# Attention denominators by accumulating DMAs, a ring of three operand tiles and more of the last inverse transform on TensorE, on one Trainium2 core

## The chip, the core and the metric

The kernel runs on one core of one Trainium2 chip. The profile shows five engines that work at the same time and wait for each other by semaphores: TensorE (PE, matrix products; the profile shows its weight loads as PEld), VectorE (DVE), ScalarE (ACT), GpSimd (POOL) and SyncE (SP). In the kernel before, PE, DVE, ACT and POOL are busy for 378.5, 360.7, 274.6 and 16.8 us of a span of 398.5 us. The page counts the transfers against 16 DMA engines. In this kernel SP issues almost all DMAs (228 of the 235 in the trace of before), one after the other, and an issue that waits for a semaphore holds up those behind it.

The metric is the device time of one execution in microseconds (us), lower is better. Each run here is four executions of a kernel, unless said otherwise, beside executions of the kernel before on the same chip. A ratio is the mean time of one kernel's fast runs over the mean of the fast runs of the kernel before in the same rounds, so it is not quite the ratio of the medians that are quoted. An execution is in the state "slow" when it took more than 1.5% longer than the fastest of the same kernel; ratios leave those out.

## The reference, cut to what matters

```python
# q, k, v: (4 batches, 8 heads, 768, 64); 16 centroids per head; x: (4, 768, 512)
mask   = argmax(q_n @ c_n.T)[:, None] == argmax(k_n @ c_n.T)[None, :]   # same cluster
scores = where(mask, (q @ k.T) / 8, -1e9)
p      = exp(scores - max)
attn   = p / (p.sum(-1) + 1e-9)               # <- the denominators of this study
x      = concat_heads(attn @ v)               # (4, 768, 512)
x1, x2, x3 = split(x @ w_proj, 3)
y      = x1 * irfft(rfft(x2) * rfft(filter)) * x3    # along the 768 rows
out    = y @ w_out
```

## The kernel before: the parts that matter

The kernel is not written in the order in which it runs. It describes operations (engine, estimated cost, due time, what it reads and writes), and a planner in Python orders them on every engine before anything is built. Constants of that planner (`T0`, `margin`, `b0` and others) therefore decide the order. The work is 16 pairs of heads (two heads share the 128 partitions). For each pair PE computes scores in six key tiles, ACT takes the exponential, PE multiplies with the values, and DVE adds the six exponential tiles up, so that only a sum over the 128 partitions is left for the denominators. PE does that sum by a matmul with ones:

```python
def acc(e, t=t):                                   # DVE, 1.75 us, five per pair
    T.nc.vector.tensor_tensor(T.acc[:], P_(t[0]), P_(t[1]) if len(t) == 2 else T.acc[:], op=Alu.add)
...
def den(e):                                        # PE: sum over partitions, line 691
    for hp in range(2):
        for ch in range(2):
            z = 2 * hp + ch
            T.nc.tensor.matmul(ap(h)[32 * z:32 * z + 32, :384], T.ones32,
                               T.acc[:, hp, ts(ch, 384)], start=True, stop=True)
...                                                # ACT copies to T.den, then SP, in order:
T.nc.sync.dma_start(T.dd[os], T.den[0:128:32])     # to HBM
T.nc.sync.dma_start(T.dn, T.dd[os].rearrange(...)) # back, spread over 128 partitions
T.nc.vector.reciprocal(T.dn, T.dn)                 # DVE
T.nc.sync.dma_start(T.dr[os].rearrange(...), T.dn) # to HBM
T.nc.sync.dma_start(T.rb[...], T.dr[os][hp:hp + 1].to_broadcast([64, S]))  # twice
```

`rb` then scales the value product into `xT`, the operand of the projection. The cluster mask gets into the scores as 16 extra rows of the score operands. The operand is called `aug`; its mask rows come from `ohT` (the one-hot cluster numbers, transposed) by eight small DMAs for each group of two pairs, also on SP.

```python
def masks(n, prs, due):
    ...
    op(("SP", .6), lambda e, ...: dma(e)(
        T.augs[aset][pr][hp][j][64 - 64 * hp:80 - 64 * hp], T.ohT[r0:r0 + 16]), due + .3 * hp,
        r=[("ohT", pr), ("zero", aset, pr, j)], w=[("augm", aset, pr, hp, j)], byts=25e3)
```

After the last pair follows a tail of about 50 us: the gating of the last batch, with inverse transforms (`I`) on PE whose even and odd parts DVE combines, and the output.

The softmax here doesn't subtract the row's maximum and nothing guards it: scores larger than these inputs give would overflow.

## Time and profile before

| | before |
|---|---|
| time, median of 3 (range) | 400.61 us (399.87 to 401.47) |
| profiled span | 398.5 us |
| PE busy, idle | 378.5 us, 20.0 us |
| DVE, ACT, POOL busy | 360.7, 274.6, 16.8 us |

PE is busy for 95% of the span and the chain of waits puts 89% of the span on PE. The next view cuts the span at the ends of the first, the sixth and the sixteenth pair's value products: head, pairs 2 to 6, pairs 7 to 16, tail. After each window comes its length, the busy time of each engine with its number of instructions, the granted clock, and the DMA engines' share.

```profile
0.00:44.90 44.90, 35.71 (x266) 18.88 (x268) 39.10 (x72) 33.79 (x67) 16.79 (x55) 1.00 0.93 175
44.90:133.60 88.70, 88.19 (x730) 44.87 (x727) 78.21 (x87) 72.02 (x133) 0.00 (x0) 1.00 0.48 111
133.60:348.80 215.20, 215.20 (x2033) 117.34 (x2037) 205.55 (x262) 154.41 (x292) 0.00 (x0) 1.00 0.28 75
348.80:398.50 49.70, 39.43 (x429) 23.85 (x427) 37.88 (x67) 14.36 (x27) 0.00 (x0) 0.94 0.16 65
```

From 133.6 to 348.8 us PE has no idle time that the profile shows (215.20 of 215.20), while DVE is busy for 95.5% of it. The groups of instructions give the ones-matmul (line 691; count, busy us, mean ns), and the waits of PE (total us, times, longest):

```profile
L691 PE MATMUL bank<-acc,ones 128*32 128x384 f32 x128 | 13.6, 498 | 0.0
```

```profile
PE bank L549 <- DMA qkraw<-in_q_dram: 5.1, 1, 5.1
PE bank L68 <- DVE y L860: 3.5, 2, 3.3
...
PE bank L68 <- DMA aug<-ohT: 0.4, 1, 0.4
```

Apart from a first load and one wait in the tail (for `y`, 3.3 us), PE waits for nothing over 1 us.

### The profile page before, as it was taken

What the parts mean: (1) busy time and instruction counts of PE and PEld (TensorE: products, weight loads), DVE (VectorE), ACT (ScalarE), POOL (GpSimd) and SP (SyncE); (2) the same over time, 40 slices, a digit from 0 to 9 for tenths busy, and PEclk for the clock granted to TensorE, in tenths of its full rate; (3) what the DMA queues carried; (4) which work ended last, traced back from release to release, by engine and by line L of the source; (5) the groups of instructions that cost most, each with busy time, mean ns of one, the idle gap of its engine ahead of it and who ended that gap; (6) DMA issues with size and microseconds to landing.
All of it is one profiled execution on the core that took longest, in us unless ns stands there. A gap on an engine that the chain in (4) does not pass through costs nothing.

```text
span 398.5 us, 8781 instructions
## 1 busy us (share of the span) xinstructions
PE 378.5 (95%) x3447; PEld 204.9 (51%) x3447; DVE 360.7 (91%) x485; ACT 274.6 (69%) x518; POOL 16.8 (4%) x55
## 2 busy tenths in 40 slices
PE   3988999999999999999999999999999999999963
PEld 3543555554445555665455555665455465555731
DVE  8889896996899999999799999999889999989981
ACT  5897889798865886768764886778865667532412
POOL 8700000000000000000000000000000000000000
PEclk9999999999999999999999999999999999999988
DMA  9939959154512415134712414111512010100304
GB/s 177 227 62 226 199 118 234 41 130 116 138 42 61 120 26 114 33 86 141 225 42 58 123 26 103 44 56 52 189 43 60 2 42 3 43 2 7 153 2 159
DMA packets 67233, 37.09 MB, mean 93 GB/s; under 512 B 56700, under 2 KB 62328, under 8 KB 67192
## 3 DMA queue, kind: packets, MB, share of 16 engines
q1 hardware_dynamic: 62856, 33.62, 33.5%
q0 software_dynamic: 1056, 2.10, 2.9%
q10 hardware_dynamic: 3280, 0.82, 1.2%
q8 instruction: 27, 0.44, 0.5%
q14 instruction: 14, 0.11, 0.1%
HBM read 30.66 MB, written 6.48 MB: 93 GB/s over the span
## 4 chain that ended last, share of the span: by engine, by line
PE 89%; ACT 4%; DMA 2%; DVE 2%; issue 1%; ACTq 0%; SPq 0%
PE bank L68 34%; PE pair L668 31%; PE bank L770 5%; PE bank L539 4%; PE bank L691 3%; PE bank L66 3%; PE bank L567 3%; ACT p L657 2%; PE bank L434 2%; DMA qkraw<-in_k_dram 1%; PE bank L580 1%; PE bank L549 1%; DMA aug<-ohT 1%; ACT p L654 1%; PE bank L460 1%
## 5 line engine op out<-in xcount | busy, mean ns | idle before, releaser
L668 PE MATMUL pair<-p,vraw 128*64 128x385 f32 x768 | 141.8, 490 | 1.0 <-ACT qkT L244 1.0
L657 ACT ACTIVATE p<-bank 128x512 f32<-128x512 f32 x192 | 113.3, 608 | 30.2 <-PE bank L68 26.7
L678 DVE TENSOR_TENSOR acc<-p,acc 128x1536 f32<-128x1536 f32 x64 | 112.2, 1754 | 6.6 <-ACT p L657 4.5
L668 PEld LDWEIGHTS pair<-p,vraw 128*64 128x64 f32 x768 | 52.2, 136 | 48.4 <-issue 40.9
L68 PE MATMUL bank<-aug,aug 128*64 128x256 bf16 (+3 forms) x654 | 69.9, 326 | 0.5 <-DMA aug<-ohT 0.4
L654 ACT ACTIVATE p<-bank 128x512 f32<-128x512 f32 x96 | 58.2, 606 | 3.0 <-PE bank L68 2.9
L68 PEld LDWEIGHTS <-aug 128*64 128x64 bf16 (+1 forms) x654 | 36.0, 110 | 31.5 <-issue 16.1
L68 PE MATMUL bank<-xT,wpj 128*64 128x384 bf16 x480 | 48.0, 326 | 0.0
L68 PEld LDWEIGHTS <-wpj 128*64 128x64 bf16 x480 | 26.9, 109 | 20.8 <-issue 11.5
L244 ACT COPY qkT<-bank 128x384 f32<-128x384 f32 x55 | 25.1, 485 | 16.1 <-PE bank L539 6.2
L678 DVE TENSOR_TENSOR acc<-p,p 128x1536 f32<-128x1536 f32 x16 | 28.0, 1750 | 4.4 <-ACT p L657 4.4
L244 ACT CAST aug<-qkT 64x768 bf16<-64x768 f32 x36 | 30.0, 833 | 2.5 <-DVE qkT L246 1.7
L68 PEld LDWEIGHTS <-y 128*64 128x64 bf16 x416 | 21.0, 112 | 15.6 <-issue 4.7
L794 DVE TENSOR_TENSOR tm<-bank,hm 128x512 f32<-128x512 f32 x44 | 27.9, 681 | 0.0
L68 PE MATMUL bank<-wout,y 128*64 128x512 bf16 x160 | 21.2, 405 | 3.5 <-DVE y L860 3.5
L770 PE MATMUL bank<-wpj,xT 128*64 128x512 bf16 x192 | 22.8, 379 | 0.0
L244 ACT COPY ob<-bank 128x512 f32<-128x512 f32 x18 | 10.3, 586 | 16.3 <-PE bank L68 15.4
L683 ACT COPY osb<-pair 128x770 f32<-128x770 f32 x16 | 12.8, 802 | 12.0 <-PE pair L668 11.7
L539 PE MATMUL bank<-ident,qkraw 128*128 128x128 f32 x144 | 20.0, 280 | 0.0
L539 PEld LDWEIGHTS bank<-ident,qkraw 128*128 128x128 f32 x144 | 15.5, 140 | 8.5 <-issue 4.1
L783 DVE TENSOR_TENSOR uv<-tm,bank 128x512 bf16<-128x512 f32 x24 | 15.3, 682 | 4.0 <-PE bank L770 2.1
L770 PEld LDWEIGHTS <-xT 128*64 128x64 bf16 x192 | 10.7, 110 | 10.8 <-issue 3.1
(146 smaller groups left out, 429.2 us busy)
## 6 DMA issues: line engine op xcount, KB each, us to landing
vraw<-in_v_dram SPq DMA_DIRECT2D x16, 384.0 KB
qkraw<-in_q_dram SPq DMA_DIRECT2D x30, 192.0 KB
qkraw<-in_k_dram SPq DMA_DIRECT2D x30, 192.0 KB
rb<-dr SPq DMA_DIRECT2D x30, 192.0 KB
out_dram<-ob SPq DMA_DIRECT2D x11, 512.0 KB
y<-in_moe_filter_fft_dram SPq DMA_DIRECT2D x4, 384.0 KB
wpj<-in_moe_w_proj_dram POOLq DMA_DIRECT2D x1, 1536.0 KB, 12.3
aug<-ohT SPq DMA_DIRECT2D x60, 24.0 KB
```

The costliest lines, as they stand in the source:

```text
L66: return T.nc.tensor.matmul(out, lhsT, rhs, start=start, stop=stop)
L68: T.nc.tensor.matmul(out[64 * i:64 * i + 64], lhsT[:, 64 * i:64 * i + 64], rhs, start=start, stop=stop)
L244: T.nc.scalar.copy(out, in_)
L539: T.nc.tensor.transpose(bank(h.ids[i // 3])[:, ts(i % 3, 128)], raw(s, i), T.ident)
L654: T.nc.scalar.activation(o, ap(h).rearrange("p (a b) -> p a b", a=2), Act.Exp, scale=0.125)
L657: T.nc.scalar.activation(flat(s)[:, lo:lo + 512], ap(h), Act.Exp, scale=0.125)
L668: T.nc.tensor.matmul(o[64 * hp:64 * hp + 64, ch, :385], T.vraw[vs][:, hp, sk * D:(sk + 1) * D], T.p[slots[sk]][:, hp, 384 * ch:384 * ch + ...
L678: T.nc.vector.tensor_tensor(T.acc[:], P_(t[0]), P_(t[1]) if len(t) == 2 else T.acc[:], op=Alu.add)
L683: op(("ACT", .83), lambda e: T.nc.scalar.copy(T.osb[os], two(ob)[:, :, :385]), te, r=[ob], w=[("osb", os)], free=[ob])
L770: T.nc.tensor.matmul(ap(h)[64 * i:64 * i + 64], T.xT[xs][:, kt, c:c + 64], T.wpj[:, kt, DM:2 * DM], start=kt == 0, stop=kt == ND - 1)
L783: op(("DVE", .68), lambda e, m=m, e_=e_, o_=o_, h=h: T.nc.vector.tensor_tensor(T.uv2[:, e_, m], T.tm[m % 2][:, 0], ap(h), op=o_), due + 1, ...
L794: op(("DVE", .68), lambda e, i=i, cs=cs, r=r, h=h: T.nc.vector.tensor_tensor(T.tm[r][:, cs], ap(h), hmrow(i, (0, 2, 2, 3)[2 * r + cs]), op ...
```

## The change

Its intent is to take work from the bound engine. Of the 16 ones-matmul passes 14 go: three accumulating DMAs fold the partitions from 128 to 16 (64, 32 and 16 rows are added onto the lower ones), the rest goes through HBM, and a small DVE reduction adds the 16 rows. There are two `acc`, so that the next pair's sums needn't wait, and three output copies `osb`. To make room in SBUF (the on-chip memory; the kernel's tiles there have up to 128 partitions) the score operands become a ring of three for pairs, in place of two sets of two. The planner also chains the scores, so that they stay in their own order. The weights are loaded in four quarters. In the tail PE forms the sums and differences of the inverse transform itself (doubled matmuls, with a negated table), and POOL may take some sums from DVE. The planner's constants were set anew, so that the order of PE's work differs throughout. The core of the diff:

```diff
-    T0 = 9.454
-    TAU1 = 3.31
-    TAU2 = 3.644
+    T0 = 12.158
+    TAU1 = 3.211
+    TAU2 = 3.472
+    def ring(n, pr):
+        return (2 * n + pr) % 3
 ...  (further constants: bonus, margin, shape, b0, w0, w1, LEAD, BUSY)
-        op(("PE", .68), den, te + 0.5, r=["acc", "ones"], w=[h], alloc=h, kind="den")
+        late = n == NG - 1                 # the last two pairs keep the ones-matmul
+        if late:
+            ...
+                flat_ = lambda: T.acc[os][:].rearrange("p a b -> p (a b)")
+                rows = 64
+                while rows >= ROWS:        # ROWS = 16
+                    op(("POOL", .8), lambda e, rows=rows: T.nc.gpsimd.dma_start(
+                        flat_()[:rows], flat_()[rows:2 * rows], accum_op=Alu.add), te, ...)
+                    rows //= 2
+                op(("SP", .6), lambda e: T.nc.sync.dma_start(T.dd[os], flat_()[:ROWS]), ...)
+                op(("SP", .6), lambda e: T.nc.sync.dma_start(T.dp, T.dd[os].rearrange("r (p b) -> p r b", b=12)), ...)
+                def gather(e):
+                    T.nc.vector.tensor_reduce(T.dn, T.dp[:].rearrange("p r b -> p b r"), axis=AX, op=Alu.add)
+                    T.nc.vector.tensor_scalar(T.dn, T.dn, EPS * S, None, op0=Alu.add)
 ...
-    T.augs = [[[[tl([128, S], BF16, ...) for j in range(2)] for hp in range(2)] for pr in range(2)] for i in range(2)]
+    T.augs = [[[tl([128, S], BF16, ...) for j in range(2)] for hp in range(2)] for i in range(3)]
 ...  (weights: one DMA of w_proj becomes four; tail: below)
+                if last:
+                    for cs in range(2):
+                        for g in range(2):
+                            for e_ in range(2):
+                                for n in range(2):
+                                    columns(bk(hh, cs)[...], T.y[:, 2 if n else e_, cs, ts(dt, 128)],
+                                            T.neg[:, cs, n] if e_ and g else T.inv[:, e_, cs, n], e_ + n == 0, e_ + n == 2)
+                    return
```

## The prediction

> **What bounds it now.** TensorE. The page gives PE 378.5 us busy of 398.5 (95%), DVE 360.7, ACT 274.6. By windows of 25 us, PE is 25.00 of 25 in every window from 100 to 350 us, at full clock; DVE is at 24.4 to 24.9 in the windows that hold gating work (125-175, 225-275, 300-350). The chain of waits gives PE 89% of the span. PE idles about 10 us before 100 us (loads, first masks) and about 10 us after 375 us (3.3 us waiting for DVE's y2 at 381.8-385, then copies and output DMA after the last matmul).
>
> **Removed.** The ones-matmul over partitions (L691 in the groups): 13.6 us busy in 16 passes. In the timeline a pass keeps the next matmul away for 0.78 us, and the matmuls before it run out 0.10 us later than usual[...]: 0.88 us. Fourteen of sixteen go: 12.3 us of PE. ACT loses about 14 copies of 0.49 us. In the tail DVE loses eight sums of 0.55 us and hands four of 0.68 us to POOL: 7 us.
>
> **Added.** Per pair: three accumulating DMAs (64, 32, 16 rows), two DMAs through HBM, a short DVE reduction and addition (estimate 0.45 us from the 0.55 us reduction of 384 and 0.15 us small operations; 6 us in all). In the tail the inverse sums double: four more groups of 16 matmuls, 0.65 us each, 2.6 us of PE. Costed by the built order with the trace's durations, PE work falls about 10.5 us in all, DVE about 6; DVE work up to the last attention pair is unchanged.
>
> **The DMA chain.** [...] From wout's 5.7 us to landing (512 KB) and small writes of about 2.4 us here, I estimate 25-30 us from last sum to operand. The order allows for it: between the last value product of a batch and the first projection it now holds 34-42 us of PE work, against 19-24 before. So I expect PE rarely to wait for it. The second acc keeps the sums from waiting.
>
> **On the critical path.** Nearly all 12.3 us lie where PE is saturated, but:
> - After the sixth pair the order holds about 214 us of PE and 214 us of DVE work (before: 216 and 200). DVE becomes a co-limit; I allow 2-4 us of new PE idling.
> - Tail: DVE falls by 7 us, PE work after the last value product rises from 37 to 40 us, so the tail turns PE-bound and keeps its length (±2).
> - The ring of three and weights by quarters make room and smooth loads; worth 0-2 us before 100 us (the 3.7 us mask DMA on the chain at 87 us may go).
>
> **Prediction.** 400.6 - 12.3 + 2.6 - 2 (tail wait) - 1 (head) + 3 (DVE bubbles) = 391 us; I put 390.5, range 383 to 398. Faster by over 2%: 0.62; within 2%: 0.33; slower: 0.05.
>
> **What would show it.** L691 left with two passes; PE busy near 368-370; last value product at 335-340 us (348.8 now); no large PE wait on rb or xT; DVE over 93% busy; the wait on y2 before the last projection under 2 us.
>
> **What would make it wrong.** Accumulating DMAs that take 10 us each, so that DVE waits for a free acc or PE for xT; loads stuck in SP's in-order queue behind the denominators' DMAs, or POOL's queue stuck on the filter wait (22 us now) before the first pair's accumulation[...]; more DVE bubbles than 4 us.

The sum comes to 390.9 us. The prediction took that the three accumulations run one after the other, on which its estimate of 25-30 us also rests; no trace of the kernel before shows it. In the trace of the change they do: POOL waits 116.3 us in all, 25 times, for an earlier accumulation (`acc<-acc`). POOL's sums: in the change the four took 1.27 us each.

## More of the kernel before

The page of the profile gives, in this order: busy time of each engine; the busy share in 40 slices of the span, in tenths, for PE and for the clock that PE was granted; what the software queue of DMAs carried; and the chain of work that ended last, by engine.

```profile
PE 378.5 (95%) x3447; PEld 204.9 (51%) x3447; DVE 360.7 (91%) x485; ACT 274.6 (69%) x518; POOL 16.8 (4%) x55
PE   3988999999999999999999999999999999999963
PEclk9999999999999999999999999999999999999988
...
q0 software_dynamic: 1056, 2.10, 2.9%
...
PE 89%; ACT 4%; DMA 2%; DVE 2%; issue 1%; ACTq 0%; SPq 0%
```

## The result and the profile after

| | before | after |
|---|---|---|
| time, median of 4 (range) | 401.04 us (399.87 to 401.88) | 417.27 us (416.34 to 418.74) |
| ratio, 95% interval | | 1.041 (1.0366 to 1.0454) |
| profiled span | 398.5 us | 414.9 us |
| PE busy, idle | 378.5, 20.0 us | 379.4, 35.5 us |
| DVE, ACT, POOL busy | 360.7, 274.6, 16.8 us | 358.5, 277.0, 55.0 us |

The result is correct and 4.1% slower. The same lines of the page, the same stages (ends of the first, sixth and sixteenth pair), the group of the ones-matmul and PE's waits for the kernel after:

```profile
PE 379.4 (91%) x3357; PEld 214.4 (52%) x3357; DVE 358.5 (86%) x491; ACT 277.0 (67%) x515; POOL 55.0 (13%) x102
PE   3878969997997999998999899999998999989994
PEclk9998998999999899999999999999999999989998
...
q0 software_dynamic: 3344, 11.73, 19.3%
...
PE 48%; DVE 22%; DMA 9%; ACT 7%; issue 7%; SPq 5%; ACTq 0%; DVEq 0%
```

```profile
0.00:45.50 45.50, 34.22 (x238) 18.36 (x240) 38.01 (x73) 31.04 (x60) 16.15 (x55) 0.96 0.92 178
45.50:140.10 94.60, 84.20 (x633) 44.07 (x631) 75.34 (x81) 71.57 (x130) 13.30 (x17) 0.96 0.73 138
140.10:365.00 224.90, 218.73 (x1985) 125.08 (x1983) 208.98 (x280) 159.23 (x296) 20.53 (x26) 1.00 0.56 109
365.00:414.90 49.90, 42.21 (x511) 26.88 (x507) 36.19 (x59) 15.15 (x29) 5.02 (x4) 0.93 0.19 73
```

```profile
L711 PE MATMUL bank<-acc,ones 128*32 128x384 f32 x16 | 1.7, 498 | 1.1 <-DVE acc L696 1.1
```

```profile
PE bank L72 <- DMA aug<-ohT: 7.5, 6, 2.9
PE bank L560 <- DMA qkraw<-in_q_dram: 5.9, 2, 5.5
PE bank L70 <- DMA aug<-ohT: 3.7, 2, 2.3
```

The ones-matmul did shrink from 128 records to 16, that is from 16 passes to 2. Yet PE is as busy as before, and idle for 15.5 us more. The chain of waits no longer runs on PE alone: DVE has 22%, DMA 9%, SP's queue 5%. (DVE's share is no sign of the loss: in `e5b_noaccum` below, the same order without the loss, it is 20%, with DMA at 2%.) The largest new wait of PE is for the masks, `aug<-ohT`: 7.5 + 3.7 us where there were 0.4. Against the kernel before, the time is lost from the second to the sixth pair (94.6 us against 88.7) and from the seventh to the sixteenth (224.9 against 215.2). The software queue carried 11.73 MB in place of 2.10.

The timeline of the second longest of these waits (start, duration, engine, line, operation; in brackets the idle time before it and what ended it; lines between are left out):

```profile
129.70 0.77 POOL L731 DMA_DIRECT2D acc<-acc  x1 [6.76 <-DMA acc<-acc]
130.17 4.71 SPq L456 DMA_DIRECT2D aug<-ohT  x6
...
134.64 0.76 POOL L731 DMA_DIRECT2D acc<-acc  x1 [4.17 <-DMA aug<-ohT]
134.83 0.10 PEld L70 LDWEIGHTS <-aug 80*128 80x128 bf16 x1 [2.55 <-DMA aug<-ohT]
134.87 0.38 PE L70 MATMUL bank<-aug,aug 80*128 80x512 bf16 x1 [2.34 <-DMA aug<-ohT]
```

An accumulating DMA starts at 129.70 us. The mask DMAs are issued from 130.17 us on, and PE's first score of that pair comes only at 134.87 us, after 2.34 us of idling that a mask DMA ended. The clock records of the trace grant PE half its rate (0.5) from 135.1 us for 3.413 us. Ahead of this window stood 2.34 us of wait, and 2.94 us ahead of another such window at 63.4 us; in the 3.413 us before these two windows PE was busy for 1.07 and 1.18 us. In the traces of before and after the changes of the granted clock are whole multiples of 3.413 us apart. I counted, over the 19 traces and from 26 us on, the windows of this grid at full rate by how long PE was busy in them: of 43 under 1.38 us all were followed by half rate, of 27 from 1.38 to 2.0 us 12, of 75 from 2.0 to 2.72 us 4, of 1905 above none (in before and after alone: 5 of 5, 2 of 2, 0 of 7, 0 of 201). So these two waits can each have cost up to 1.7 us more (an estimate: half of 3.413 us); of the eight waits for masks in this trace, these two were followed by such a window.

How tight is the order? From the built order of PE and mean durations from the trace I worked out how much PE work stands between the transposes that make `ohT` and the first score that needs the masks made of it, for the seven groups of two pairs:

```
us of PE work    g1    g2    g3    g4    g5    g6    g7
before         21.8   6.2  12.6   8.2  13.6   8.1  12.5
after          12.2   4.9   6.0   4.9   5.7   5.7   8.5
```

Into that time must fit a copy of `ohT` (0.99 us on ACT), up to eight mask issues (0.59 us each) and the landing of the last one. Four issues with the copy and a landing of 1.9 us (the median without accumulations, below) are 5.3 us by this estimate: in five of its seven groups the order after has next to no reserve, so that a landing of 3 us, or an issue that is held, shows as idle PE.

### The profile page after: what moved, and what is told of

Same layout as the page of the kernel before. It is cut to its first block, busy times and chain, and to the rows that moved or that the text cites. A ratio compares the mean times of both kernels' runs of the same rounds, so it can differ in the third digit from the quotient of the medians.

```text
span 414.9 us, 8661 instructions
## 1 busy us (share of the span) xinstructions
PE 379.4 (91%) x3357; PEld 214.4 (52%) x3357; DVE 358.5 (86%) x491; ACT 277.0 (67%) x515; POOL 55.0 (13%) x102
## 3 DMA queue, kind: packets, MB, share of 16 engines
q1 hardware_dynamic: 90060, 36.20, 38.1%
q0 software_dynamic: 3344, 11.73, 19.3%
## 4 chain that ended last, share of the span: by engine, by line
PE 48%; DVE 22%; DMA 9%; ACT 7%; issue 7%; SPq 5%; ACTq 0%; DVEq 0%
PE bank L72 17%; PE pair L682 15%; DVE acc L696 8%; DMA aug<-ohT 5%; PE bank L809 4%; SPq L456 4%; PE bank L70 3%; PE bank L550 3%; DVE tm L833 2%; ACT p L671 2%; PE bank L579 2%; DMA qkraw<-in_q_dram 2%; DVE xT L777 1%; ACT aug L255 1%; DMA rb<-dr 1%
## 5 line engine op out<-in xcount | busy, mean ns | idle before, releaser
L682 PE MATMUL pair<-p,vraw 128*64 128x385 f32 x768 | 147.5, 500 | 1.6 <-DVE inv L257 1.1
L696 DVE TENSOR_TENSOR acc<-p,acc 128x1536 f32<-128x1536 f32 x64 | 111.7, 1745 | 5.4 <-ACT p L671 2.8
L682 PEld LDWEIGHTS pair<-p,vraw 128*64 128x64 f32 x768 | 56.0, 139 | 51.5 <-issue 44.5
L72 PE MATMUL bank<-aug,aug 80*64 80x512 bf16 (+3 forms) x602 | 72.1, 330 | 9.2 <-DMA aug<-ohT 7.5
L731 POOL DMA_DIRECT2D acc<-acc x42 | 33.6, 800 | 274.3 <-DVE acc L696 144.8
L72 PEld LDWEIGHTS <-aug 80*64 80x64 bf16 (+1 forms) x602 | 37.0, 110 | 39.4 <-issue 25.0
L72 PEld LDWEIGHTS <-wpj 128*64 128x64 bf16 x480 | 28.7, 109 | 17.8 <-issue 8.9
L72 PEld LDWEIGHTS <-y 128*64 128x64 bf16 x472 | 23.0, 110 | 12.8 <-issue 4.5
L70 PE MATMUL bank<-aug,aug 80*128 80x512 bf16 (+3 forms) x83 | 19.3, 322 | 6.4 <-DMA aug<-ohT 3.7
L257 DVE COPY qkT<-bank 128x384 f32<-128x384 f32 x18 | 9.5, 553 | 12.7 <-PE bank L550 12.7
L777 DVE SCALAR_TENSOR_TENSOR xT<-osb,rb 128x768 bf16<-128x768 f32 x15 | 15.2, 1014 | 5.7 <-DMA rb<-dr 5.6
```

The source lines that it names most:

```text
L70: return T.nc.tensor.matmul(out, lhsT, rhs, start=start, stop=stop)
L72: T.nc.tensor.matmul(out[64 * i:64 * i + 64], lhsT[:, 64 * i:64 * i + 64], rhs, start=start, stop=stop)
L682: T.nc.tensor.matmul(o[64 * hp:64 * hp + 64, ch, :385], T.vraw[vs][:, hp, sk * D:(sk + 1) * D], T.p[slots[sk]][:, hp, 384 * ch:384 * ch + ...
L696: T.nc.vector.tensor_tensor(T.acc[os], P_(t[0]), P_(t[1]) if len(t) == 2 else T.acc[os], op=Alu.add)
L731: op(("POOL", .8), lambda e, rows=rows: T.nc.gpsimd.dma_start(flat_()[:rows], flat_()[rows:2 * rows], accum_op=Alu.add), te, r=[], w=[("ac ...
L777: op(("DVE", .6 if last else 1.05), lambda e, a_=a_: T.nc.vector.scalar_tensor_tensor(xv()[:, a_], osv()[:, a_], eps(), ap(rk[a_.start])[: ...
```

## The experiments

Three theories to start with:
- A, order: the new planner constants put the masks too late, whatever the DMAs do.
- Q, queue: SP is held by the waits of the denominators' chain, and the masks stand behind them.
- C, contention: the accumulating DMAs load the DMA engines, and the masks land later.

"Same order" below means that the order of PE, DVE and ACT was checked to be that of the parent kernel, so that nothing else moved. Several kernels give a wrong result.

### 1. Orders planned anew (five kernels, none settled it)

`e1_margin` sets one constant of the planner back (`margin` from 0.005 to 0.43), `e4_masks_earlier` plans the clusters 8 us earlier (`b0 = end - 31.5`), and `e2_den_on_pe` brings the ones-matmul back for all pairs:

```diff
-        late = n == NG - 1
+        late = True
```

> Edit: the changed kernel with the scheduler's margin for TensorE back at 0.43 us (it is 0.005 in the change). In the built order the PE work between the transposes of a head group's one-hot rows (ohT) and the first score of that group grows from 4.9-12 us (mostly under 6) to 8-24 us. Theory A (the new order leaves no slack between ohT, eight serial mask DMAs and the scores that need them[...]): PE idle falls from 35 us towards 20 us, the half-rate windows inside the span go, time 388 to 398 us. Theory B (mask DMAs are held in SP's in-order queue by the denominators' DMAs that wait for their chain) and theory C (traffic of the accumulating DMAs slows the masks and loads): the chain and traffic stay, so time stays at 410 us or more.

> Edit: the changed kernel with all denominators summed by matmuls with ones, as before the change (no accumulating DMAs, no dp, no gather); ring, score chain, quarters, tail and constants as in the change. PE work rises by 12 us. The scheduler, given this, leaves 6 to 15 us of PE work between ohT and the first score. A, B and C all expect it to be faster than the changed kernel in spite of the added PE work: 398 to 406 us, PE wait on mask DMAs under 5 us in all. If it stays at 412 us or more, the loss lies in the ring, the score chain, the quarters or the constants, not in the denominators' DMAs.

> Edit: the changed kernel with one constant moved: routing similarities are due 8 us earlier (end - 31.5 for end - 23.515). The built order then holds 6.6 to 16 us of PE work between ohT and the first score (4.9 to 12 in the change). Theory A: time 395 to 407 us and mask waits under 8 us. Theories B and C: within 1% of the changed kernel, 413 to 420 us.

Measured, all correct: 420.25 us (ratio 1.0533), 421.94 us (1.0545) and 427.54 us (1.0664). None came out as theory A expected. e4 missed every range; e1's time lies in the range named for the other two theories (410 us or more); e2 took the branch "412 us or more", which by its own words lays the loss on the ring, the score chain, the quarters or the constants. I don't read it so: e5b below keeps all of these in the unchanged order and takes 397.92 us. In e1 and e4 PE's waits for masks did fall, to 0.2 and 1.6 us, and both kernels were slower than the change: theory A lost its support as the whole cause. Other waits appeared in their place, for exponentials above all (6.1 us in e1, 6.3 in e4 on line 72). In e2 PE waited 7.6 us once for a table of the gating and 8.9 us for `y`, and the tail took 61.3 us instead of 49.9. What follows is a lesson of method: each of these edits made the planner reorder everything, and the new order brought losses of its own that are as large as the effect in question.

Two later kernels say the same. `e9_old_consts` is the change with all planner constants of before; `e8_den_pe_old_consts` is that with the ones-matmul back as well, so that of the change only the ring of three, the three copies, the weights by quarters and the tail stay.

> The change without its DMA denominators: ring of three operand tiles, three output copies, weights by quarters and the new tail stay, the denominators of every pair are summed on PE as before, the planner's constants are those of before. Correct result. If ring, quarters and copies cost nothing and gain nothing, this is as the tail alone: 395-399 us, L691 again in 16 passes, ohT to first score with 9 to 14 us of PE work between, mask waits under 2 us. If the ring of three itself makes the mask waits (a tile is free later), 402-410 us with aug<-ohT among PE's waits above 5 us.

> The whole change with the planner's constants of before; correct result; PE order differs: PE work between the transposes of ohT and the first score that needs it is 28, 47, 37, 5.5, 5.1, 5.5, 5.1 us for the seven head groups (after: 12.2, 4.9, 6.0, 4.9, 5.7, 5.7, 8.5). Theory (contention and queue act only where an order is tight): no PE wait on masks over 0.5 us in groups 1 to 3, waits of 1 to 3 us in some of groups 4 to 7, time 403-415 us. Rival (the new constants are what is wrong, not the DMAs): no waits on masks over 1 us at all, time 388-398 us.

Measured, both correct: e8 418.91 us (1.0469), e9 436.69 us (1.0904). In e8 there is no accumulating DMA and PE doesn't wait for masks, but 8.3 us once for a table on DVE and 5.7 us in the tail for `y`. In e9 PE waited 4.8 us for masks and more for exponentials (7.0 us in one group alone), so neither theory's number came. e8's time is outside both of its ranges too. From here on I only changed kernels without letting the order move.

### 2. Queue and contention, in the unchanged order after (four cells)

`e3_no_chain_waits`: the chain's DMAs on SP copy constant data, so that SP waits for nothing in the chain; the accumulating DMAs stay.

```diff
-  T.nc.sync.dma_start(T.dd[os], flat_()[:ROWS])
+  T.nc.sync.dma_start(T.dd[os], T.wpj[:ROWS, :2]...)       # likewise dp, dr, rb
```

`e5b_noaccum`: the 42 accumulating DMAs are left out, the chain's waits stay (and a constant added to the sums becomes 1.0). `e5_no_waits_no_accum`: both edits.

```diff
-  op(("POOL", .8), lambda e, rows=rows: T.nc.gpsimd.dma_start(..., accum_op=Alu.add), te, ...)
+  op(("POOL", .8), lambda e: None, te, ...)
```

> Edit: the changed kernel, same order of instructions on every engine, but the four kinds of denominator DMA on SP copy constant data (weights, q) in the same shapes, so that SP never waits for the accumulation, the gather or each other; wrong result on purpose. Theory B: masks and loads get out earlier, PE wait on masks falls to under 5 us, time 395 to 406 us. Theory A: the masks wait mostly for ohT itself and for their own eight serial issues, so time falls by less than a third of the loss, 409 to 416 us. Theory C: traffic stays, 412 to 418 us.

> Edit: the previous run without waits (e3), and the 42 accumulating DMAs left out as well; same order of instructions on every engine; wrong result on purpose. Theory C (traffic of the accumulating DMAs slows masks, loads and weight of everything else): a further gain of 4 us or more over e3 (409.95), to 397-405 us. Theory B (only the waits on SP's queue count): same as e3 within 1%, 406 to 412 us.

> Fourth cell of the two by two (SP's chain waits with/without, accumulating DMAs with/without), same order on every engine as after, wrong result on purpose: the 42 accumulating DMAs are left out, SP keeps its waits for the chain dd, dp, dn, dr, rb. Contention theory (the accumulating traffic lengthens the mask DMAs' landings): median landing of aug<-ohT falls from 3.0 us to about 2 us, and the time falls by about as much as between the two kernels without chain waits (12.6 us), to 403-406 us. Queue theory (SP is held behind the chain whatever the traffic): mask landings fall but PE still waits for masks 5 us or more in all, time 408-412 us. If the queue is held mainly because the accumulations make the chain slow, the two overlap: time 397-402 us, mask waits under 2 us.

| ratio to before (95% interval) | accumulating DMAs | none |
|---|---|---|
| SP waits for the chain | 1.041 (1.0366 to 1.0454), the change | 0.9946 (0.9917 to 0.9974), e5b |
| SP doesn't wait | 1.0216 (1.0166 to 1.0265), e3 | 0.9915 (0.9888 to 0.9943), e5 |

The medians are 417.27 and 397.92 us in the first row, 408.69 (three fast runs; the fourth, 416.64, was slow) and 397.37 us in the second. The trace gives the landing of the mask DMAs, from issue, as minimum, median and maximum of those it could match (44 of 60 in each). In the order after, e3, e5b, e5:

```profile
DMA to landing us min/median/max: 1.8/3.0/8.4
```

```profile
DMA to landing us min/median/max: 1.8/3.1/7.4
```

```profile
DMA to landing us min/median/max: 1.8/1.9/3.6
```

```profile
DMA to landing us min/median/max: 1.8/1.9/3.6
```

And the queue's own waits, first of the kernel after, then of e5b (SP's queue, what it waited for, total us, times, longest):

```profile
SPq L745 <- DVE dn L744: 57.4, 12, 9.8
SPq L737 <- DMA dd<-acc: 30.0, 12, 3.8
```

```profile
SPq L744 <- DVE dn L743: 64.7, 12, 10.9
SPq L736 <- DMA dd<-acc: 23.6, 12, 3.3
```

What follows:
- The accumulating DMAs are what makes the change slow in this order: without them it takes 4.5% less time (ratio 1.041 to 0.9946), whether or not SP waits it ends below the kernel before, and the view of PE's waits shows none for masks (it leaves out gaps under 0.15 us). e5b has PE idle for 21.4 us, where the change has 35.5. By stages, with the order unchanged, 12.9 of the 18.7 us lie in pairs 2 to 6 and 5.1 in pairs 7 to 16 (e5b in the view that was used above):

```profile
46.50:128.20 81.70, 79.78 (x633) 42.84 (x631) 72.41 (x78) 70.33 (x130) 0.00 (x0) 1.00 0.53 115
128.20:348.00 219.80, 217.84 (x1987) 122.44 (x1983) 211.01 (x284) 158.63 (x297) 0.00 (x0) 1.00 0.36 84
```

- They act as contention: the mask landing is 1.9 us without them and 3.0 or 3.1 us with them, and that doesn't depend on SP's waits. The loads of `vraw` and `q` land later too (medians 4.4 and 3.7 us in e5b, 5.3 and 4.4 in the change). The page of the change counts the software queue, which carries the accumulations, and the largest hardware queue against the same 16 DMA engines (19.3% and 38.1% of their time; in e5b 2.9% and 39.5%); how the transfers share them, no view here shows. A slower DVE is no rival: the same running sums take a mean of 1745 ns in the change and 1746 in e5b (DVE is busy for 358.5 and 357.1 us in all).
- Part of it is not the accumulations' own traffic. POOL too issues its DMAs one after the other, and the second accumulation of the first pair, which waits 7.36 us for the first, holds back two of the four quarters of the weights:

```profile
39.00 0.89 POOL L731 DMA_DIRECT2D acc<-acc  x1 [19.64 <-DVE acc L696]
40.43 1.14 POOL L1002 DMA_DIRECT2D wpj<-in_moe_w_proj_dram  x2 [0.30 <-POOL wpj L999]
48.94 0.85 POOL L731 DMA_DIRECT2D acc<-acc  x1 [7.36 <-DMA acc<-acc]
49.49 1.42 POOL L1002 DMA_DIRECT2D wpj<-in_moe_w_proj_dram  x2
```

  These two land at 56.9 and 61.0 us, beside the masks of the first group, five of which take 6.6 to 8.4 us; the longest wait of PE (2.94 us) and the half-rate window at 63.4 us follow. In e5b all four quarters are issued from 40.4 to 42.0 us and no mask of that group takes over 3.4 us. Over the later groups the median landing of the masks is still 2.9 us (the longest 4.8) against 1.9, and 8.0 of the 11.2 us of waits remain. No run separates the two shares.
- The queue alone costs almost nothing: 0.3% without accumulations, which the intervals don't tell from zero, though SP waits for the chain as long as in the change (64.7 + 23.6 us against 57.4 + 30.0). It costs 1.9% only together with the accumulations. The two causes are not additive, and I had expected 403 to 406 us for e5b from contention alone; the time and the mask waits of the third case came. Its reason, a queue held because the accumulations make the chain slow, is not what these two waits of the queue show, for they are as long without accumulations.

The same place in the timeline of e5b, for comparison with 130.17 to 134.87 us above:

```profile
120.21 3.75 SPq L456 DMA_DIRECT2D aug<-ohT  x6
...
124.06 0.53 SPq L744 DMA_DIRECT2D dr<-dn  x1
124.63 1.98 SPq L456 DMA_DIRECT2D aug<-ohT  x2
124.67 0.38 PE L70 MATMUL bank<-aug,aug 80*128 80x512 bf16 x1
```

The first six issues take 3.75 us in place of 4.71 and the score at 124.67 us has no wait ahead of it.

### 3. Two more looks at the masks

`e6_masks_const`: in the change, the mask DMAs copy a constant tile instead of `ohT`, so that they don't wait for the clusters (same order, wrong). `e13_chain_on_pool`: `dd`, `dp`, `dr` and `rb` are issued by POOL, with a correct result.

> Edit: the changed kernel, same order on every engine, with the mask DMAs copying a constant table instead of ohT, so that SP issues them without waiting for the one-hot rows; wrong result on purpose. Chain and traffic of the denominators stay. Theory A2 (the visible loss is 13 us of PE waits on the mask DMAs and 7 us of half clock that follows the longest of them): PE waits on aug<-ohT under 3 us, at most one half-rate window before the tail, time 396 to 405 us. Theory B (SP is held by the denominators' DMAs, whatever it waits for at the masks): masks still late, 409 to 416 us.

> after with dd, dp, dr and rb issued by POOL and not by SP, so that SP's queue carries no chain wait; PE, DVE and ACT in the same order; correct result; accumulating traffic stays. Queue theory: as with constant data in the chain, SP free, mask waits shrink by some 5 us, time 408-412 us, unless POOL's chain becomes late: then PE waits on xT or DVE on acc and rb appear instead, over 3 us each, and the time stays at 415-425 us. Contention alone predicts no change: 415-419 us with the same mask waits.

e6 took 409.55 us (ratio 1.0214), in the range of the queue theory. That is about as much less than the change as e3 gained: the waits of the mask issues for `ohT` are worth as much as the waits of the chain, and with either gone some 2% is left beside the traffic. PE's matmuls still waited 5.6 us for masks (4.2 + 1.4 us in the view of waits), whose median landing was 3.2 us: even masks that depend on nothing come late behind what holds the queue, and under this traffic. e13 had one fast run (416.88 us) and three slow ones (423.73 to 427.24 us), so it has no ratio. No gain from moving the chain to POOL shows: the one fast run takes as long as the change, and in the profile, which is of a slow execution, waits for `xT` and `uv` appear beside the masks.

### 4. The same traffic where the order has room

`e10_traffic`: the kernel before, in its own order, with 42 accumulating DMAs of 64, 32 and 16 rows added on POOL, after each of the first 14 pairs, into a scratch tile that nothing reads (1328 of 1536 columns; there was no room for more). The result is correct.

```diff
+  for rows in (64, 32, 16):
+      T.nc.gpsimd.dma_start(T.scr[:rows], T.scr[rows:2 * rows], accum_op=Alu.add)
```

> Edit: the kernel before the change, same order on PE, DVE, ACT and SP, with the 42 accumulating DMAs added on POOL into a scratch tile (1328 of 1536 columns, all the room there is), each set started by the output copy; denominators as before, result correct. Theory C: DMA contention[...] slows the rest: 404 us or more. Otherwise within 0.5% of before: 399 to 402.5 us.

It took 404.33 us, ratio 1.0071 (1.0031 to 1.0111): about 3 us, at the lower edge of theory C's range. The traffic as such is not worth 19 us. The change differs from e10 in that PE stands some 5 us behind the masks, that a chain waits on the traffic, and that two weight loads wait behind it; which of these makes the difference was not separated.

### 5. The tail alone

`e7_tail_alone`: the kernel before with only the tail of the change: doubled inverse sums on PE, eight DVE sums fewer, POOL allowed for the sums of `y`. PE's order is that of before up to the tail.

```diff
+  for e_ in range(2):
+      for n in range(2):
+          columns(bk(hh, cs)[...], T.y[...], T.neg[:, cs, n] if e_ and g else T.inv[:, e_, cs, n], e_ + n == 0, e_ + n == 2)
```

> Edit: the kernel before the change with only the tail's part of the change (inverse sums doubled on PE, eight DVE sums less, four sums offered to POOL); the order on PE is the same as before up to the tail. If the tail's part pays as the change intends: 394 to 398.5 us. If it is neutral (PE work for DVE work): 399 to 402 us. If POOL's sums or the added matmuls cost: 402 us or more.

It took 397.08 us, correct, ratio 0.9912 (0.9883 to 0.9942). It beats the kernel before by less than 2% (and the change by more). The tail shrank from 49.7 to 46.4 us, and the wait of 3.3 us for `y` is gone from PE's waits. So the gain of e5 and e5b against before, 0.5 to 0.9%, is no more than the tail alone gives. On balance the removal of 14 passes seems to have brought nothing, even without accumulations. The stages say that this is a sum of gains and losses of the new order and not the tail's gain again: e5b takes 81.7 us for pairs 2 to 6 (88.7 before), 219.8 for pairs 7 to 16 (215.2) and 48.2 for the tail (49.7). What the removal is worth was open, and the next runs ask.

### 6. The removal alone, in the order of before

`e11_no_den`: the kernel before without the 14 passes and with nothing else changed; the copy that follows reads a slice of `acc` in SBUF (wrong). `e12_tail_no_den` adds the tail, `e14_traffic_no_den` adds the traffic of e10.

```diff
 def den(e):
+    if n < NG - 1:
+        return
 def total(e):
+    src = lambda: ap(h)[:, :384] if n == NG - 1 else T.acc[:, 0, :384]
```

> before, with the 14 ones-matmul passes of the first 14 pairs left out and nothing else (the copy that follows reads a slice of acc in SBUF, so the result is wrong on purpose); same order on PE, DVE, ACT and SP. Theory O (the re-planned order spent the gain; the removed work was on the critical path): the time falls by 9 to 12 us, to 388-391 us, PE busy 366-369 us, the last value product at 337-340 us. Rival D (DVE and ACT are co-limits that swallow it): the time falls by less than 5 us, to 395-399 us, PE idle grows by 7 us or more, with waits on DVE and ACT of 0.3 to 1 us.

> The tail alone (397.1 us, faster than before by 3.5 us) with the same 14 passes left out, same order otherwise, wrong on purpose. Theory O: 384.5-388 us, that is, the two gains add up. Rival D: 392-396 us.

> e11 with the 42 accumulating DMAs into a scratch tile on POOL (1328 of 1536 columns), as in the run that added this traffic to before (+3 us there): wrong on purpose. If an order with room for the masks keeps the cost of the traffic small also when PE has less work: e11 + 3, 391-395 us under theory O. If the shorter PE order loses that room: e11 + 6 or more, with PE waits on aug<-ohT over 2 us.

e11 took 396.13 us, ratio 0.9888 (0.9846 to 0.9929): 1.1%, some 4.5 us. e12 took 393.85 us, 0.9823 (0.9782 to 0.9864); e14 403.23 us, 1.0041 (0.9983 to 1.0099). The stages of e11, cut as before:

```profile
PE 369.2 (94%) x3335; PEld 210.5 (53%) x3335; DVE 359.8 (91%) x485; ACT 274.6 (70%) x518; POOL 16.8 (4%) x55
```

```profile
44.10:130.80 86.70, 85.39 (x698) 44.73 (x695) 76.78 (x86) 71.93 (x133) 0.00 (x0) 1.00 0.50 114
130.80:344.30 213.50, 209.83 (x1961) 122.88 (x1965) 205.57 (x262) 154.52 (x292) 0.00 (x0) 1.00 0.28 76
```

PE's busy time fell by 9.3 us, but its idle time rose from 20.0 to 24.9 us. From the seventh pair on, where PE had been busy for 215.20 of 215.20 us, it is now busy for 209.83 of 213.50, though 9 of the 14 passes stood there. So rival D of the expectation, that something swallows the work taken away, is right in time (its idle time was to grow by 7 us or more; it grew by 4.9), and the reading "PE is saturated here" was wrong. e12 shows that removal and tail about add up: together they give 1.8% in the order of before. In e14 the traffic costs 1.5% on top of e11, against 0.7% on top of before. That it costs more once PE has less work is only just clear of the intervals, and the waits don't explain it: DVE waits 7.7 us for `rb` and PE once 2.0 us for a mask, but in e10 these are 6.6 and 1.9 us.

I also summed, over all PE matmuls of each trace, the time from the start of one to the start of the next, by what the first of the two works on. This is my own reckoning from the trace's start times:

```
us               before    e11    e7   e5b   after
ones x acc         12.5    1.6  12.5   2.2     2.2
scores             69.8   73.0  70.0  77.7    88.2
value products    128.5  129.8 129.6 130.1   132.2
inverse            10.8   10.6  13.4  14.4    14.4
```

In e11, of the 10.9 us that the passes took, 3.2 reappear behind scores and 1.3 behind value products; the rest of what was not gained is spread over small groups that are not shown. In e5b, the change without accumulations, 7.9 us more stand behind scores than in before, by this reckoning most of what the removed passes freed. Seven of these steps are over 0.6 us, 6.3 us in all (before: two, 2.1 us); the rest is spread thin. Why the new order has them was not tested. In the change itself the scores take another 10.5 us.

### 7. Is VectorE what swallows it?

`e15_one_sum_less` leaves out one of the five DVE sums in each of the first 14 pairs (24.5 us of DVE) in the kernel before; `e16_no_den_one_sum_less` does so in e11. Both are wrong, in the same order.

```diff
 def acc(e, t=t):
+    if n < NG - 1 and t == (3,):
+        return
```

> before, with one of the five running sums on DVE left out in each of the first 14 pairs (14 times 1.75 us, 24.5 us of DVE; result wrong on purpose, same order). If PE is the only bound of before: no change, 399-401 us. If DVE already costs PE some waits in before: 397-399 us. Below 396 us neither reading of before holds.

> The run without the 14 ones-matmul passes (396.1 us) with the same 14 DVE sums left out as well, wrong on purpose. Theory D (DVE is the co-limit that swallowed the gain): the rest of the gain appears, 387-391 us, PE idle falls from 24.9 to 20-21 us, no PE waits on DVE sd, tm, oh. Rival A (chains through ACT and the buffers): 394-396 us, PE idle stays at 24 us or more.

e15 took 400.28 us, ratio 0.9983 (0.9959 to 1.0007): no change that could be told from none. So DVE, as far as these sums go, costs nothing in the kernel before. e16 took 394.63 us, 0.9831 (0.9801 to 0.9862), against 0.9888 for e11: about 2 us, which the intervals only just tell from zero, in line with pairs 7 to 16, which took 210.9 us in its profile against 213.5. So DVE seems to hold back some of the gain, but theory D in its strict form (387 to 391 us, PE idle down to 20 to 21 us) missed. The time is in the range of rival A, whose idle time (24 us or more) missed as well:

```profile
PE 369.8 (94%) x3335; PEld 210.0 (53%) x3335; DVE 336.8 (86%) x471; ACT 274.2 (70%) x518; POOL 16.8 (4%) x55
```

PE is idle for 22.9 us there. About 4 us of the 10.9 remain unaccounted for by DVE. The chain of waits of e16 spreads over DVE 14%, DMA 6% and ACT 6%, and I did not separate these. What swallows that part is left open.

## Why the prediction was wrong

It said 390.5 us, within 383 to 398, with 5% for slower by over 2%. It was 417.27 us. Point by point:

- "PE is bound", and removing 14 passes leaves two: right. 16 records are left, and e15 shows that DVE did not bind.
- "Nearly all 12.3 us lie where PE is saturated": wrong as a count of time to be gained, and this is the first step that failed. The passes took 10.9 us, and taking them alone away gave 1.1%, some 4.5 us. I had read 25.00 busy of 25 us as work that will turn into time. Busy time promised more than there was: PE looked fully busy (215.20 of 215.20 us) in the stage in which only 1.7 us were gained (215.2 to 213.5) for 9 passes.
- "The DMA chain ... So I expect PE rarely to wait for it": the step that cost most. The literal statement held, for PE hardly waits for `xT` or `rb`. But I had set the chain's length against the room that its own result has, 34 to 42 us. I had not set its traffic and its waits against the room of the other DMAs: the masks have 5 to 6 us of PE work in five of seven groups, and they share the SP queue with the chain, whose accumulations the page counts against the same 16 DMA engines (19.3% of their time for that queue). With accumulations their median landing was 3.0 us, without 1.9 us, PE waited 11.2 us for masks in place of 0.4, and the change took 19 us longer than the same order without accumulations. "Loads stuck in SP's in-order queue" was named among what could go wrong, but the runs show that the queue alone costs 0.3%, within noise; it took the accumulations as well.
- The accumulating DMAs mostly stayed far below the 10 us that I had feared: their median landings were 5.5, 4.2 and 3.7 us for 384, 192 and 96 KB (the longest, the first, 9.7 us), with 0.8 us of POOL for each issue. The 25 to 30 us from last sum to operand was too low: by the trace's start and end times it took 34 to 52 us over the 14 pairs, and 33 to 46 us in e5b, so that most of it is not the accumulations. It isn't what cost the time, for PE hardly waited for the operand.
- "The tail keeps its length (±2)", and a wait on `y2` that goes: half right. In the change the tail took 49.9 us (49.7 before), but alone it saved 3.3 us, the wait it was meant to remove. What took that back in the change was not separated.
- "2-4 us of new PE idling" from DVE: the mechanism is there (e11 against e16: about 2 us), but it was a fraction of 15.5 us of new idling, and DVE's share fell to 86%, where I had expected over 93%.
- PE busy 368 to 370 us and the last value product at 335 to 340 us: wrong, 379.4 us and 365.0 us. Part of it seems to be PE at half rate (granted clock 0.5 for 3.413 us at 63.4 and at 135.1 us): PE was busy for 374.8 us in e5b in the same order, with no half-rate window between the first loads and the tail (granted clock 1.00 from 46.5 to 348.0 us).

What no run shows is a correct kernel with these denominators in an order that has room for the masks and no new losses. The nearest, e14, has the traffic and no chain behind it, and is not faster than before. A planned order that gives the masks room might cost something elsewhere; the planned orders that I tried all did.

## What to carry to other kernels

Before adding DMAs to a kernel, look for the small transfers with the least slack and for the loads that will queue behind the new ones, not only for the room that the new transfers' own result has: here PE waited 11.2 us for transfers of 24 KB with some 5 us of room, and the removed PE work was worth 4.5 us. A fully busy PE row doesn't say how much time removed PE work will give; leave the work out in the unchanged order first (a wrong result is fine for that), because that one run showed 4.5 us where 12.3 had been counted. And where a planner orders the program, an experiment that lets it plan anew measures the new order, not the edit.
